# From a greedy schedule to a fixed order of all engines, with idle matmuls between the matmuls of the first two batches

## The chip, the cores and the metric

The kernel runs on one core of one Trainium2 chip. The metric is the device time of one execution in microseconds, as a median of several runs; lower is better. The engines are named as in the profile: PE (matmuls), PEld (its weight loads), DVE (vector), ACT (activations), POOL (GpSimd), SP (issues transfers). The kernels put matmul results into eight banks of PSUM, the accumulator memory. A run is called slow here when it is over 1.5% above the fastest run of the same kernel. Medians and ranges are of all runs; ratios and their intervals are of fast runs alone.

## The reference

Eight batches of eight heads: linear attention with an exponential feature map, then a gated unit with a causal convolution over five steps. The heart of it:

```python
def phi(x):                                    # x: (8, 8, 576, 64), w_phi: (64, 128)
    proj = np.einsum('bhsd,df->bhsf', x, w_phi)
    proj = proj - np.max(np.abs(proj), axis=-1, keepdims=True)
    return np.concatenate([np.exp(proj), np.exp(-proj)], axis=-1)
kv  = np.einsum('bhsf,bhsd->bhfd', phi(k), v)  # state
z   = np.sum(phi(k), axis=2)
x   = num / den                                # phi(q) kv / (phi(q) z + 1e-6), to (8, 576, 512)
gate = sigmoid(sum of 5 shifted x, each times conv_w[k])
out = (gate * (x @ w_val)) @ w_out             # (8, 576, 512) float32
```

## The kernel before

Every piece of work is a task with an engine, a duration from a table and a list of tasks it needs. A greedy scheduler simulates the engines when the kernel is built: whenever an engine is free, it takes the ready task of lowest priority number and, if the task opens a PSUM group, the first free bank or pair of banks.

```python
def run(self):                       # (cut)
    ...
    for e in engs:
        if free[e] > now + 1e-9:
            continue
        best = None
        for i in pend[e]:
            t = tasks[i]
            ...
            if best is not None and tasks[best].prio <= t.prio:
                continue
            g = t.grp
            if g is not None and t.opens:
                if nlive.get(g.kind, 0) >= self.live.get(g.kind, 8) or find(g.nb) is None:
                    continue
            best = i
    ...
    if e == "PE" and t.mode != mode:
        dur += 0.03
        mode = t.mode
```

The pieces that the change rewrites are the scaling of V by the k maxima on POOL (with masked copies where a block of rows straddles two heads), the state products, the gate, and the loads:

```python
def vs(self, t, b, g, s):            # POOL; (cut)
    for side in range(2):
        nc.gpsimd.tensor_tensor(EM[...], EK[...], MASK[...], ALU.mult)
    for a, st, n in ((1, 2, 4), (0, 8, 2)):
        nc.gpsimd.tensor_tensor(VT[:, s, sl, :, 0:D], Vg[:, sl, :, :], e..., ALU.mult)
    for side in range(2):
        nc.gpsimd.tensor_tensor(VB[:, s, :, :, side, 0:D], Vg[:, 2:7:2, :, :], e..., ALU.mult)

def rows(self, w, b):                # a 512-byte piece of q, k or v for each partition and y
    return self.src[w][b].rearrange("h (r t) d -> (h r) (t d)", t=2).rearrange("(y p) c -> p y c", p=P)
```

## Time and profile before

| | before |
|---|---|
| time, median (range) | 260.82 us (257.94 to 261.92) |
| profiled span, mean clock | 259.5 us, 0.916 |
| first exponential starts, last ends | 14.7, 231.1 us |
| first normalization of x in full blocks starts, last ends | 59.95, 238.5 us |

The lines that carry the reading stand in the prediction below. One more belongs here, the chain of work that ended last, by engine:

```profile
PE 52%; DMA 30%; DVE 10%; POOL 3%; issue 2%; ACT 1%; DVEq 0%; ACTq 0%; POOLq 0%
```

Three tenths of what set the end was data arriving: a load and transposing transfers of q.

### The profile page before, as it was taken

The numbers are of one execution on the slowest core, as the hardware profiler recorded it, in microseconds if no ns is written. First come the engines' busy times: TensorE is split into PE (matmuls) and PEld (weight loads), VectorE is DVE, ScalarE is ACT, GpSimd is POOL, SyncE is SP. The second block draws the span as 40 slices with busy tenths as digits, with TensorE's granted clock in tenths as the row PEclk, the third lists the DMA queues.
The fourth block names the chain that finished last, engine by engine and source line by source line (L and its number), as shares of the span: only waits on it lengthen the run. The fifth ranks groups of instructions, "written<-read, shape, count | busy, mean of one in ns | idle before, by whom it ended". The sixth has DMA issues, their size and how long they took to land.

```text
span 259.5 us, 8486 instructions
## 1 busy us (share of the span) xinstructions
PE 211.5 (81%) x3550; PEld 154.5 (60%) x3572; DVE 179.1 (69%) x284; ACT 187.1 (72%) x275; POOL 167.5 (65%) x364
## 2 busy tenths in 40 slices
PE   0464275588999999899984999899969999999982
PEld 0452153476776577667763677567747776677640
DVE  3373572687789888987893779877968799348320
ACT  1183389289888899898983898799869988563332
POOL 8880099799977797879494596767475747930000
PEclk9996555559999999999998899999999999999998
DMA  7999999999959996999999949981972002302205
GB/s 182 203 216 196 148 182 171 170 192 141 169 54 164 174 207 101 142 221 120 197 124 183 156 104 139 209 212 20 145 120 83 3 3 98 111 3 83 81 26 179
DMA packets 95760, 35.24 MB, mean 136 GB/s; under 512 B 84842, under 2 KB 91114, under 8 KB 95722
## 3 DMA queue, kind: packets, MB, share of 16 engines
q0 software_dynamic: 52624, 14.55, 57.3%
q1 hardware_dynamic: 42848, 20.06, 42.4%
q8 instruction: 28, 0.46, 0.8%
q10 hardware_dynamic: 250, 0.09, 0.1%
q14 instruction: 10, 0.08, 0.1%
HBM read 31.54 MB, written 9.44 MB: 158 GB/s over the span
## 4 chain that ended last, share of the span: by engine, by line
PE 52%; DMA 30%; DVE 10%; POOL 3%; issue 2%; ACT 1%; DVEq 0%; ACTq 0%; POOLq 0%
DMA qT<-KQN 20%; PE PS L754 12%; DMA KQN<-in_q_dram 10%; PE PS L775 9%; PE PS L742 8%; PE PS L551 7%; PE PS L621 6%; PE PS L663 3%; PE PS L668 2%; DVE GV L760 2%; DVE XN L708 2%; PE PS L716 2%; DVE MQP L558 2%; DVE GVT L765 1%; PE PS L684 1%
## 5 line engine op out<-in xcount | busy, mean ns | idle before, releaser
L568 ACT ACTIVATE KTIL<-PS 128x1024 bf16<-128x1024 f32 (+1 forms) x80 | 73.3, 943 | 12.0 <-PE PS L551 9.6
L674 ACT ACTIVATE QTIL<-PS 128x1024 bf16<-128x1024 f32 (+1 forms) x80 | 73.2, 947 | 11.7 <-PE PS L668 11.7
L558 DVE TENSOR_REDUCE MQP<-PS 128x8 f32<-128x1024 f32 (+1 forms) x40 | 44.1, 1114 | 17.4 <-PE PS L551 16.3
L588 POOL TENSOR_TENSOR VT<-VN,EK 128x512 bf16<-128x512 bf16 x64 | 53.3, 833 | 0.0
L593 POOL TENSOR_TENSOR VB<-VN,EM 128x384 bf16<-128x384 bf16 x64 | 52.7, 824 | 0.0
L558 DVE TENSOR_REDUCE MK<-PS 128x8 f32<-128x1024 f32 (+1 forms) x40 | 44.2, 1109 | 3.8 <-ACT KTIL L568 3.7
L754 PE MATMUL PS<-XT,WV 64*128 64x288 bf16 x512 | 37.1, 283 | 0.4
L760 DVE SCALAR_TENSOR_TENSOR GV<-TH,PS 128x576 bf16<-128x576 bf16 x32 | 24.1, 752 | 18.6 <-PE PS L754 15.7
L582 POOL TENSOR_TENSOR EM<-EK,MASK 128x6 f32<-128x6 f32 x64 | 11.4, 197 | 37.5 <-ACT EK L574 37.5
L775 PE MATMUL PS<-WOUT,GV 128*128 128x512 bf16 x106 | 30.8, 387 | 5.3 <-DVE XN L708 2.7
L635 ACT ACTIVATE OUTS<-PS 128x512 f32<-128x512 f32 x31 | 18.5, 597 | 17.7 <-PE PS L775 10.0
L621 PEld LDWEIGHTS <-KTIL 128*128 128x128 bf16 x640 | 27.7, 103 | 5.0 <-issue 3.3
L742 PE MATMUL PS<-XT,GT 128*64 128x288 bf16 x384 | 29.7, 290 | 0.0
L754 PEld LDWEIGHTS <-WV 64*128 64x128 bf16 x512 | 24.7, 94 | 7.5 <-issue 2.9
L746 ACT ACTIVATE TH<-PS 128x576 bf16<-128x576 f32 x32 | 21.2, 663 | 7.3 <-PE PS L742 5.6
L551 PE MATMUL PS<-W,qT 64*128 64x128 bf16 x288 | 17.4, 240 | 10.4 <-DMA qT<-KQN 8.6
L621 PE MATMUL PS<-VB,KTIL 128*128 128x130 bf16 (+1 forms) x256 | 22.0, 216 | 1.2 <-POOL VB L595 1.2
L708 DVE TENSOR_TENSOR XN<-PS,RCP 128x512 bf16<-128x512 f32 x32 | 22.1, 691 | 1.1
L742 PEld LDWEIGHTS <-GT 128*64 128x64 bf16 x384 | 18.9, 109 | 6.6 <-issue 3.2
L621 PE MATMUL PS<-VT,KTIL 128*128 128x65 bf16 x384 | 22.3, 200 | 0.5 <-ACT QTIL L674 0.5
L551 PE MATMUL PS<-W,kT 64*128 64x128 bf16 x288 | 16.0, 235 | 7.9 <-DMA kT<-KQN 4.6
L551 PEld LDWEIGHTS <-qT 64*128 64x128 bf16 x288 | 10.7, 104 | 18.0 <-DMA qT<-KQN 9.3
(64 smaller groups left out, 297.7 us busy)
## 6 DMA issues: line engine op xcount, KB each, us to landing
out_dram<-OUTS SPq DMA_DIRECT2D x32, 256.0 KB, 3.7
VN<-in_v_dram POOLq DMA_DIRECT2D x8, 576.0 KB, 11.8
KQN<-in_k_dram POOLq DMA_DIRECT2D x7, 576.0 KB, 9.6
KQN<-in_q_dram POOLq DMA_DIRECT2D x7, 576.0 KB, 15.4
QTIL<-in_k_dram SPq DMA_DIRECT2D x4, 256.0 KB, 4.1
WV<-in_moe_w_val_dram POOLq DMA_DIRECT2D x2, 512.0 KB, 14.0
QTIL<-in_q_dram SPq DMA_DIRECT2D x4, 256.0 KB, 12.1
out_dram<-OUTS SPq DMA_DIRECT2D x16, 64.0 KB, 2.3
```

Of the source, the lines that this page charges most:

```text
L551: nc.tensor.matmul(self.PS[:, t.grp.bank + par, i * P:(i + 1) * P], X[rows, (c0 + i) * P:(c0 + i + 1) * P], self.W2[rows, :], start=True, ...
L558: self.nc.vector.tensor_reduce(o, self.PS[:, t.grp.bank:t.grp.bank + 2, 0:n * P].rearrange("p a (c f) -> p a c f", f=F), AX.X, ALU.max, ap ...
L568: self.nc.scalar.activation(self.KTIL[b % 2][:, s, :, c0 * P:(c0 + n) * P], self.PS[:, t.grp.bank:t.grp.bank + 2, 0:n * P], AF.Exp, scale= ...
L588: nc.gpsimd.tensor_tensor(VT[:, s, sl, :, 0:D], Vg[:, sl, :, :], e.unsqueeze(3).to_broadcast([P, n, 2, D]), ALU.mult)
L593: nc.gpsimd.tensor_tensor(VB[:, s, :, :, side, 0:D], Vg[:, 2:7:2, :, :], e.unsqueeze(3).to_broadcast([P, 3, 2, D]), ALU.mult)
L621: nc.tensor.matmul(ps[:, col:col + E1 * len(mine)], self.KTIL[b % 2][:, s, par, c * P:(c + 1) * P], rhs, start=first, stop=True, skip_grou ...
L674: self.nc.scalar.activation(o, self.PS[:, t.grp.bank:t.grp.bank + 2, 0:n * P], AF.Exp, scale=1.0 - 2.0 * s)
L708: nc.vector.tensor_tensor(o.rearrange("p (g h) d -> p g h d", g=ng), n[:, :, :, 0:D], rc.unsqueeze(3).to_broadcast([P, ng, 4, D]), ALU.mult)
L742: nc.tensor.matmul(self.PS[h2 * D:(h2 + 1) * D, t.grp.bank + par, 0:R], self.GT[:, h, par, s, :], X[:, h, 2 - s:2 - s + R], start=(s == 0) ...
L754: nc.tensor.matmul(self.PS[:, t.grp.bank + par, 0:R], self.WV2[rows, h, j * P:(j + 1) * P], X[rows, h, 2:2 + R], start=(h == 0), stop=(h = ...
L760: nc.vector.scalar_tensor_tensor(out=self.GV[b % 3][:, j, :, :], in0=self.TH[j][:, :, :], scalar=1.0, in1=self.PS[:, t.grp.bank:t.grp.bank ...
L775: nc.tensor.matmul(self.PS[:, t.grp.bank, :], lhsT, self.WOUT[:, j, :], start=(j == 0), stop=(j == 3))
```

## The change

The intent of the last step, which gives the change its name, is to keep PE's clock up while the first two batches wait for data, by matmuls whose result nobody reads. The diff holds much more. The greedy scheduler gives way to fixed lists (an order of all tasks on all engines, a bank for each group, an engine for each movable copy), found offline. Cut to its core:

```diff
-PRM = dict(T=19.98, kp=(0.65, 4.21), ...)          # priorities
-LIVE = dict(kp=3, qm=2, ...)
+ORDER = ("15 16 18 17 20 19 22 21 24 35 23 37 ... ")  # 1064 tasks, all engines
+FLEX = ("ADAADAAAAAPPAPPD ... ")                      # ACT, DVE or POOL
+BANKS = ("460006544445500124166757 ... ")
+WARM = ("8:7:5 21:7:1 214:5:1 ")                      # place : bank : how many
...
-    def run(self):
-        ...                                           # greedy
+    def follow(self):
+        ...
+        return [self.tasks[int(i)] for i in ORDER.split()]
...
+    for i in range(NW):                               # 14 tasks of two idle matmuls
+        A("warm", 0, i, "PE", 0.44, fn("warm2"), [], plan.group("warm", 1), 0)
+    def warm(self, bank):
+        self.nc.tensor.matmul(self.PS[:, bank, :], self.ONES[:, 0:P], self.ONES[:, :], start=True, stop=True)
...
 def rows(self, w, b):
-    return self.src[w][b].rearrange("h (r t) d -> (h r) (t d)", t=2).rearrange("(y p) c -> p y c", p=P)
+    if w == "q":
+        return self.src[w][b].rearrange("h t d -> (h t d)").rearrange("(p x) -> p x", p=P)
+    return self.src[w][b].rearrange("(hp ab) (p j) d -> (ab p) hp (j d)", ab=2, j=9)
...
 def vs(self, t, b, g, s):                             # V: one product, no masks
+    eng.tensor_tensor(self.VT[g][:, s, :, 0:D], self.VN[b % 2][:, NC * g:NC * g + NC, :], e.to_broadcast([P, NC, D]), ALU.mult)
+    eng.tensor_copy(self.VT[g][:, s, :, D:E1], e)
...
 def st(self, t, b, g, x):                             # state: 64-row pairs, 144 a batch for 80
+    for ab in range(2):
+        rows = slice(ab * D, (ab + 1) * D)
+        nc.tensor.matmul(..., self.KTIL[b % 2][rows, s, J // 2, J % 2, :], self.VT[g][rows, s, 9 * x + j, :], ...)
```

Beside these: each of the gate's four parts takes 8 matmuls on the full height and half the width of the array (128 rows by 64 columns) and 4 on a quarter (64 by 64) instead of 12 of the former; V is loaded uncast through SP; the transposes of the convolution taps move behind the first k maxima; small copies on POOL hold back later loads; batch 1's q and k are transposed on PE; batches 6 and 7 transpose x by DMA; two load buffers instead of three, six output buffers instead of four.

## The prediction

> **What bounds the kernel now.** The few words that name the change fit only its last step; the diff replaces most of the kernel. So I first ask where 260 us go, starting with the page.
>
> ```profile
> span 259.5 us, 8486 instructions
> PE 211.5 (81%) x3550; PEld 154.5 (60%) x3572; DVE 179.1 (69%) x284; ACT 187.1 (72%) x275; POOL 167.5 (65%) x364
> ...
> ACT  1183389289888899898983898799869988563332
> ...
> PEclk9996555559999999999998899999999999999998
> DMA  7999999999959996999999949981972002302205
> ...
> DMA packets 95760, 35.24 MB, mean 136 GB/s; under 512 B 84842, under 2 KB 91114, under 8 KB 95722
> ```
>
> No engine is full: four lie between 167 and 212 us. ACT is thin in the first nine and last six slices, the TensorE clock is half in slices 5 to 9, and the DMA engines are full until three quarters of the span, with tiny packets. The busy-time windows put sizes on it (columns: PE, PEld, DVE, ACT, POOL busy, clock, DMA share, GB/s):
>
> ```profile
> 10.00:20.00 10.00, 7.42 (x65) 5.83 (x64) 7.75 (x18) 6.63 (x9) 7.30 (x4) 1.00 1.22 216
> 20.00:30.00 10.00, 4.64 (x38) 2.91 (x38) 5.07 (x6) 4.62 (x8) 0.00 (x0) 0.57 1.42 186
> 30.00:40.00 10.00, 5.84 (x67) 3.85 (x67) 5.58 (x7) 6.89 (x10) 7.03 (x16) 0.50 1.99 163
> 40.00:50.00 10.00, 4.31 (x57) 3.56 (x59) 3.47 (x4) 5.14 (x8) 8.21 (x20) 0.50 1.45 169
> ...
> sum 140.00, PE 128.02 PEld 94.12 DVE 114.67 ACT 119.54 POOL 103.95; mean PE 18.29 PEld 13.45 DVE 16.38 ACT 17.08 POOL 14.85
> ```
>
> The last line sums 60 to 200 us: there PE is busy 91% and ACT 85%. Before 60 us ACT works only 32.8 us (the rows above, 1.28 before and 8.27 after), so 27 are lost; after 200 us it works 34.7 of 59.5, so 25 more. The waits and the timeline say what the start waits for:
>
> ```profile
> PE PS L488 <- DMA cw<-in_moe_conv_w_dram: 9.7, 1, 9.7
> ...
> 15.89 3.81 ACT L568 ACTIVATE KTIL<-PS 128x1024 bf16<-128x1024 f32 x4
> ...
> 32.95 1.28 POOL L536 DMA_DIRECT2D KQN<-in_q_dram  x1 [14.12 <-DMA kT<-KQN]
> ```
>
> PE's first instruction stands behind a load of convolution taps until 9.7 us, though the timeline shows the k load issued at 0.74 us, and its issues land in about 4. POOL, which scales V, sits 14 us behind the transpose of the next k. In the chain of waits, 30% of the span is DMA (26.7 us of a q load from 8.2, then 12.2 of its transpose). By 47 us batch 0 has no state product; its first normalization comes at 60. In the middle it is a balance of engines under a greedy order. These groups price the work (busy, then mean ns):
>
> ```profile
> L568 ACT ACTIVATE KTIL<-PS 128x1024 bf16<-128x1024 f32 x64 | 64.5, 1029 | 10.7 <-PE PS L551 8.4 <-DVE MK L558 2.2
> L568 ACT ACTIVATE KTIL<-PS 128x512 bf16<-128x512 f32 x16 | 9.5, 595 | 1.3 <-PE PS L551 1.2
> L588 POOL TENSOR_TENSOR VT<-VN,EK 128x512 bf16<-128x512 bf16 x32 | 33.7, 1053 | 0.0
> L588 POOL TENSOR_TENSOR VT<-VN,EK 128x256 bf16<-128x256 bf16 x32 | 19.6, 613 | 0.0
> ```
>
> **What the Trainium skill says.** "TensorE: Matmul & The Clock Gate", Part 1: the array clock halves after about 3.4 us of idling and returns after as long a busy window. The trace agrees: 0.50 between 30 and 50 us, where PE is busy 43 to 58%, and 1.00 in the busy stretch after 60. The same page, Part 3: matmuls on different row or column groups of the array run concurrently. It agrees: 16 value matmuls of 64 rows and 288 columns take 0.99 us in the chain, 62 ns each, where one of 512 columns takes 216 to 240. "DMA: Bandwidth & Descriptors", Specifications: at least 512 B is needed for line rate. Here 89% of packets (84842 of 95760) are smaller, and the engines are full at about 190 GB/s. "GPSIMD Engine Reference", 3.1: about 2.6 cycles an element at 1.2 GHz for two inputs on GpSimd. Here (1053-613)/256 = 1.72 ns, 2.1 cycles; I use the measured slope.
>
> **The change part by part.** Counts are from the two compiled instruction orders.
>
> *Start.* The tap transposes go behind the first batch's k maxima, POOL's loads wait for the fourth k load, V comes uncast through SyncE and q, k in long rows (q 9.2 KB a partition instead of 512 B). PE can start transposing k when it has landed, near 4 us, not 10.65; ACT near 5.5, not 11.8: 6 us. Batch 1's q and k are transposed on PE rather than by DMA. I expect most of the other 20 lost microseconds of the start to go too.
>
> *Idle matmuls.* 35 of 128x512: five ahead of PE's first transposes, one in the first projections, 28 as 14 pairs in the ordered list between the matmuls of batches 0 and 1, one more behind them. At 0.22 us each (the pace of the 512-column output matmuls) they are 7.7 us of PE, mostly in holes. They buy clock: in the chain, PE pieces from 47 to 59 us, some 9 us at half speed, would have been about 4.5 shorter, an upper bound since batch 0 waits more for data.
>
> *ACT* (the x4 row: (3.81-1.03)/3 = 0.93 us from start to start, 0.10 less than a duration). 128 wide exponentials x 0.93 = 119; 16 half ones x 0.50 = 8; 32 quarter ones (estimate from the slope, 0.28) = 9; 32 tanh x 0.56 = 18; 22 of 36 output evictions x 0.50 = 11 (31 before); KV copies, EK and start copies about 10. Sum 175, against 181 counted so before. ACT's gain is in its idle time, not its work.
>
> *DVE.* 64 wide reductions x 1.12 = 72, 16 half ones 9, gated products 21, normalization 27, x copies 12, 24 evictions 14, the rest 8: 163. The gather copies of q and output remainders leave it.
>
> *POOL.* V is scaled in one product of 1152 elements: 1152 x 1.72 + 173 = 2.15 us plus a copy of 0.2, 31 times = 73; loads, taps, halo and gather copies about 35. So 108 instead of 167; no longer a rival.
>
> *PE per batch*, from chain and timeline pieces at full clock: projections 72 in eights of 0.33 = 3.0; q features 2.5; state 3.1; numerator 2.4; x transposes 1.35; gate 4 x 0.86 = 3.4; value 4 x 1.0; output 18 x 0.23 = 4.1; the rest 0.2: 24. Changed: state products go from 80 (64 of 65 columns, 16 of 130) to 144 half-height ones of 65 columns in concurrent pairs: 72 x 0.03 (the numerator's pace, 48 in 1.4 us) = 2.2, say 2.3; gate from 12 to 8 full plus 4 quarter-array ones, 0.86 x 8/12 + 0.12 = 0.69, so 2.8. New: 22.6 a batch, 181 in all, less 2 where batches 6 and 7 transpose x by DMA, plus 7.7 idle.
>
> *Order.* A fixed list with fixed PSUM banks replaces the greedy scheduler. The list puts all exponentials before the last stretch; after the last q features, PE still has about 0.6 state, 5.5 gate, 2.7 numerator, 8 value and 8 output: 25 us.
>
> **The sum.** ACT starts at 5.5, does 175 less about 7 in the tail = 168, with 6% idle = 10 (15% before); then PE's 25 less 2.5 overlapped by the last exponentials; then eviction 0.6 and landing 2.0: 5.5+168+10+22.5+2.6 = 208.6. PE check: 179 real microseconds between 4.5 and 206 is 89%, as in the old middle (91%), so it fits. I say **208 us**, 20% less.
>
> **Rivals.** (1) Data still comes late: 12 big DMA transposes remain, and in the old trace they take 10 to 14 us to land. Against: that was under saturation, and short packets go. If so, the start loses 10 again and the period stays DMA-bound: 220 to 225. (2) A fixed list is only as good as its timings: one late operation stalls a whole in-order queue, and ACT, PE and DVE now have nearly equal loads (175, 187, 163). At the old 15% idle ACT gives 227. For it: no slack between equals; against: the banks and engines were chosen together. (3) The idle matmuls lie on PE's path, or fail to hold the clock: 3 to 5 us more. (4) The order is tight and ACT loses 2%: 201; with less tail 198. A slower kernel would need the DMA change to fail outright; nothing speaks for it.
>
> **Range and chances.** (4) bounds the low side, most of (1) and (2) the high side: 198 to 220 holds eight in ten. Within 2% of 260 would take 47 us of error, so faster 0.98, same 0.01, slower 0.01.
>
> **What would show it.** Right: first k transposes before 6 us and first exponential before 8; PEclk 9 in slices 3 to 9; packets well under 95760, DMA below 9 in the middle; ACT busy about 175 to 180 of its span, 93% until its last exponential; POOL under 120; the last q exponential about 25 us before the end, PE full after it. Wrong: ACT windows at 85% in the middle with waits on PE (rival 2) or on qT, kT transposes (rival 1); a clock still half in the first quarter (rival 3); a tail over 30 us.

## The result, and the profile after

The changed kernel took 230.04 us in the median (229.07 to 230.28, four runs) beside 260.82 us for the kernel before. The ratio is 0.8845, with a 95% interval of 0.8761 to 0.8929. Ratios here are the mean time of one kernel's fast runs over that of the other's of the same rounds, so not quite the ratio of the medians. The direction was right. The time lies outside the predicted range of 198 to 220, and 22 us above the predicted 208.

First the page of the changed kernel, the lines that answer to those shown of before:

```profile
span 228.5 us, 9138 instructions
PE 205.4 (90%) x4001; PEld 142.6 (62%) x4027; DVE 176.3 (77%) x264; ACT 180.7 (79%) x266; POOL 102.8 (45%) x158
...
ACT  2995999889899988988899999979988999913220
...
PEclk9997999999999999999999999999999999999998
DMA  6999943999699939995899995969964206156156
...
DMA packets 49282, 39.87 MB, mean 174 GB/s; under 512 B 33690, under 2 KB 38554, under 8 KB 49178
...
PE 53%; DVE 17%; DMA 4%; issue 3%; ACT 3%; POOL 2%; DVEq 0%; ACTq 0%
```

The start is repaired: ACT is busy from the second slice on, the clock is up in all but the fourth slice until the last, packets are half as many, and data is 4% of the chain that ended last, not 30%. DMA is still at 9 in many slices, though, and that did not hurt.

Next, the first and the last normalization of x in full blocks, first the two of before, then the two of after (start, duration, engine, line):

```profile
59.95 0.69 DVE L708 TENSOR_TENSOR XN<-PS,RCP 128x512 bf16<-128x512 f32 x1
...
237.85 0.69 DVE L708 TENSOR_TENSOR XN<-PS,RCP 128x512 bf16<-128x512 f32 x1
```

```profile
40.70 0.69 DVE L691 TENSOR_TENSOR XN<-PS,RCP 128x512 bf16<-128x512 f32 x1
...
202.66 0.69 DVE L691 TENSOR_TENSOR XN<-PS,RCP 128x512 bf16<-128x512 f32 x1
```

These split the gain of the profiled spans, 259.5 - 228.5 = 31.0 us. Up to the first normalization 19.2 are won. From the first to the last start it took 177.9 us before and 162.0 after: 15.9 more. From there to the end it took 21.6 before and 25.8 after: 4.2 lost again. (Their sum, 30.9, is the gain but for rounding.)

The busy-time windows of after (PE, PEld, DVE, ACT, POOL busy, then clock, DMA share, GB/s) show the stages:

```profile
0.00:20.00 20.00, 13.35 (x133) 8.41 (x134) 11.99 (x15) 13.49 (x22) 8.49 (x17) 0.97 0.92 265
20.00:40.00 20.00, 17.12 (x333) 10.68 (x336) 14.27 (x18) 18.42 (x26) 14.40 (x24) 0.95 0.73 152
40.00:60.00 20.00, 16.87 (x410) 12.64 (x409) 17.63 (x27) 17.46 (x26) 11.63 (x14) 1.00 1.11 198
60.00:180.00 120.00, 115.96 (x2383) 82.46 (x2391) 102.53 (x155) 107.28 (x156) 56.72 (x81) 1.00 0.86 187
```

From 60 to 180 us ACT is busy 89.4%, not the 93% expected, while PE is busy 97% by the records. ACT's longest waits from 60 us to its last q exponential at 198.2 us (waiting engine and line, what ended the wait, then us in total, times, longest):

```profile
ACT TH L743 <- PE PS L739: 3.4, 8, 0.7
ACT KTIL L572 <- PE PS L555: 2.6, 5, 1.1
ACT QTIL L657 <- PE PS L649: 2.4, 7, 0.6
```

All name PE: its gate, its projections and its q features. With two smaller ones it is 10.5 us on PE, of the 13.8 that ACT is idle in this stretch. No wait of any engine is put down to a transfer there. The tail itself, from ACT's last q exponentials over PE's last output products:

```profile
194.31 3.88 ACT L657 ACTIVATE QTIL<-PS 128x1024 bf16<-128x1024 f32 x4
```

```profile
221.31 1.89 PE L775 MATMUL PS<-WOUT,GV 128*128 128x512 bf16 x8
```

The exponentials end at 198.2 us, PE ends at 223.2, and the span 5.3 us later.

**How full PE really was.** The records of matmuls overlap (in run 14 a 64-column one lasts 0.19 us and the next starts 0.01 us after it), so a PE that waits a little can look full. Starts are better. I went through PE's tasks in the trace, priced each at the shortest start-to-start time of its kind, added 0.1 us wherever PE passed between forms (half rows, full array, half columns; the reason comes with the experiments), and counted no task for longer than it took. So reckoned, PE was occupied 18.2 us of the first 35 (52%), 17.9 of the next 25 (72%), and 108.5 of the 120 from 60 to 180 (90%). This is an estimate, and the trace lacks some records, 6 of the 35 idle matmuls among them. A recount by groups of like matmuls, on this trace and that of run 5, gives 21 to 26 us of the first 35 (16 to 19 without the idle matmuls), 18 of the next 25 and 107 to 110 of the 120.

### The profile page after: what moved, and what is told of

Read it like the earlier page. It is cut to its first block, busy times and chain, and to the rows that moved or that the text cites. A ratio compares the mean times of both kernels' runs of the same rounds, so it can differ in the third digit from the quotient of the medians.

```text
span 228.5 us, 9138 instructions
## 1 busy us (share of the span) xinstructions
PE 205.4 (90%) x4001; PEld 142.6 (62%) x4027; DVE 176.3 (77%) x264; ACT 180.7 (79%) x266; POOL 102.8 (45%) x158
## 4 chain that ended last, share of the span: by engine, by line
PE 53%; DVE 17%; DMA 4%; issue 3%; ACT 3%; POOL 2%; DVEq 0%; ACTq 0%
PE PS L751 13%; PE PS L775 10%; PE PS L732 7%; PE PS L598 5%; PE PS L555 5%; DVE XN L691 4%; DMA kT<-KQN 4%; DVE MQP L562 3%; PE PS L670 3%; DVE MK L562 3%; PE PS L739 3%; DVE GV L757 2%; PE PS L642 2%; PE PS L699 2%; PE PS L649 2%
## 5 line engine op out<-in xcount | busy, mean ns | idle before, releaser
L588 POOL TENSOR_TENSOR VT<-VN,EK 128x1152 bf16<-128x1152 f32 x31 | 65.8, 2123 | 60.2 <-ACT EK L581 50.8
L657 ACT ACTIVATE QTIL<-PS 128x1024 bf16<-128x1024 f32 x64 | 62.6, 1036 | 4.6 <-PE PS L649 4.0
L751 PEld LDWEIGHTS <-WV 64*128 64x128 bf16 x512 | 24.6, 94 | 8.3 <-issue 2.6
L598 PE MATMUL PS<-VT,KTIL 64*128 64x65 bf16 x1152 | 24.1, 191 | 1.4 <-POOL VT L589 0.5
L598 PEld LDWEIGHTS <-KTIL 64*128 64x128 bf16 x1152 | 21.3, 95 | 4.2 <-issue 1.3
L670 PE MATMUL PS<-KV,QTIL 128*128 128x65 bf16 x512 | 20.1, 193 | 1.7 <-DVE GV L757 0.5
L670 PEld LDWEIGHTS <-QTIL 128*128 128x128 bf16 x512 | 18.2, 97 | 5.0 <-issue 2.7
L612 ACT ACTIVATE OUTS<-PS 128x512 f32<-128x512 f32 x22 | 13.3, 606 | 9.8 <-PE PS L775 9.1
L732 PE MATMUL PS<-XT,GF 128*64 128x288 bf16 x256 | 20.6, 290 | 0.4 <-DVE MQP L562 0.2
L775 PEld LDWEIGHTS <-GV 128*128 128x128 bf16 x128 | 11.0, 97 | 11.6 <-issue 1.1
L642 PE MATMUL PS<-qT,W 64*128 64x512 bf16 (+1 forms) x80 | 15.0, 359 | 0.9 <-ACT QTIL L657 0.5
```

The costliest lines, as they stand in the source:

```text
L588: eng.tensor_tensor(self.VT[g][:, s, :, 0:D], self.VN[b % 2][:, NC * g:NC * g + NC, :], e.to_broadcast([P, NC, D]), ALU.mult)
L598: nc.tensor.matmul(self.PS[:, t.grp.banks[ab], (s * 2 + x) * E1:(s * 2 + x + 1) * E1], self.KTIL[b % 2][rows, s, J // 2, J % 2, :], self.V ...
L657: self.nc.scalar.activation(o, i, AF.Exp, scale=1.0 - 2.0 * s)
L670: nc.tensor.matmul(self.PS[:, t.grp.banks[h // 4], (h % 4) * E1:(h % 4 + 1) * E1], Q[:, s, c % 2, h, (c // 2) * P:(c // 2 + 1) * P], self. ...
L732: self.nc.tensor.matmul(self.PS[h2 * D:(h2 + 1) * D, t.grp.banks[par], 0:R], self.GF[:, h, i, :], X[:, h, :, HALO - 8 * s:HALO - 8 * s + X ...
L751: nc.tensor.matmul(self.PS[:, t.grp.banks[par], 0:R], self.WV2[rows, h, j * P:(j + 1) * P], X[rows, h, :, HALO:XW], start=(h == 0), stop=( ...
```

## The experiments

Eighteen kernels ran. Unless said, each is the changed kernel with one edit, and is compared with its 230.0 us.

### Idle matmuls

**1. No idle matmuls.** `warm` returns at once; order and banks stay.

```diff
     def warm(self, bank):
+        return
```

> The changed kernel without its 35 idle matmuls, nothing else touched (right result). If they hold the clock and batches 0 and 1 need it: the clock drops to a half in the first quarter and the time rises by 3 to 5 us. If they only lie on PE's path: the time falls by up to 5 us. If both balance or neither matters: within 1 us of 230. My guess is 232.

Measured: 232.42 us (231.44 to 233.37), ratio 0.9003 (0.8919 to 0.9086), about 2 us longer. The windows of this kernel, then one of the changed kernel:

```profile
30.00:40.00 10.00, 5.49 (x174) 4.65 (x167) 5.37 (x7) 8.94 (x14) 6.17 (x6) 0.76 0.40 102
40.00:50.00 10.00, 8.85 (x183) 7.47 (x184) 9.09 (x18) 7.66 (x12) 6.01 (x9) 0.73 1.13 209
```

```profile
30.00:40.00 10.00, 8.18 (x220) 5.58 (x222) 6.66 (x8) 10.00 (x15) 6.72 (x7) 1.00 0.31 75
```

The idle matmuls hold the clock at 1.00 where it would be 0.73 to 0.76. They are worth 2 us of the 31 that the whole change gains.

**2. Idle matmuls in the kernel before.** One 512-column idle matmul goes ahead of each of the first 45 PSUM groups.

```diff
+            if left and t.eng == "PE" and t.opens and t.fn is not None:
+                left -= 1
+                em.idle(t.grp.bank)
```

> The kernel before with one idle matmul ahead of each of the first 45 PSUM groups that PE opens, its order untouched (right result). If the half clock cost the old start 4 us, as I put it at most: 2 to 4 less and the clock full before 50 us. If the old start waits for data: within 1, whatever the clock.

Measured: 264.05 us, ratio 1.0079 (0.9983 to 1.0175). The clock rose from 0.916 to 0.958 and the time did not fall. That fits a start that waits for data.

### Is it the order?

**3. The new operations under the old scheduler.** The changed kernel's tasks, no idle matmuls, ordered by the greedy scheduler with the old priorities.

```diff
-        for i, t in enumerate(plan.follow()):
+        for t in plan.run():         # with PRM, LIVE and the run() of the kernel before
```

> The operations of the changed kernel, without idle matmuls, ordered by the greedy scheduler and the priorities of the kernel before (right result). If the fixed order carries the gain: near the old 85% of ACT with the new start, 240 to 255. If the changed operations and loads carry it and the order little: within 5 us of 230.

Measured: 291.7 us, ratio 1.1287 (1.1169 to 1.1406). The same operations without idle matmuls take 232 us (run 1) or 292 according to their order, their banks and the engines chosen for movable copies. (The priorities were tuned for the old operations, so this is no fair verdict on greedy scheduling.)

**4. One part alone in the kernel before.** The tap transposes move behind the first k maxima.

```diff
-    cc = A("mqt", 0, 0, "PE", 0.5, fn("c_cw"), (), g, prio=-500)
+            cc = A("mqt", 0, 0, "PE", 0.5, fn("c_cw"), [G("kmax", 0, 4)], g, prio=-500)
```

> The kernel before, with its tap transposes behind the first batch's k maxima as in the changed kernel (right result). If PE's late start costs what I counted: 4 to 6 us less than before. If the start is held by q, V and the next batch's loads anyway: 0 to 2 us less.

Measured: 269.81 us, ratio 1.0453 (1.0349 to 1.0557). The first exponential came at 8.5 us instead of 14.7, and yet the kernel is slower: the greedy order reshuffled itself around the edit (ACT's instructions differ in 194 of 275 places). Which part of the new order costs the time isn't shown. Parts of this change can't be added up one by one under that scheduler.

### Which engine's work counts?

In each of these an engine's work is cut, with a wrong result where said.

**5. The changed kernel again**, as a partner for the next ones.

> The changed kernel again, unaltered, so that it stands beside the next three on the same chip: 229 to 231 us.

Measured: 230.31 us (230.21 to 231.39), ratio 0.895 (0.8893 to 0.9006).

**6. Value products over four of eight heads** (wrong result): 16 us less for PE.

```diff
-        for h in range(H):
+        for h in range(H // 2):
```

> The changed kernel with the value product over 4 of 8 heads (wrong result on purpose): 256 matmuls, 16 us, less on PE, 2.5 of them in the tail per batch 7 and 6 groups. If PE binds throughout: 14 to 16 us less. If no engine binds and hand-offs in the fixed order do: 5 to 9 less, about half of it in the tail.

Measured: 223.07 us, ratio 0.8652 (0.8557 to 0.8746): 7 us shorter, less than half of what was taken away, which is what was expected "if no engine binds". In the profiled run, the slowest of the four, the last q exponential ends at 195.3 us instead of 198.2: 2.9 us earlier, though six of eight batches, some 12 of the 16 us, lie before it.

**7. Maxima over half the features** (still within the tolerance): 38 us less for DVE.

```diff
-            o, ...rearrange("p a (c f) -> p a c f", f=F),
+            o, ...rearrange("p a (c f) -> p a c f", f=F)[:, :, :, 0:F // 2],
```

> The changed kernel with the k and q maxima over half of the features (wrong result on purpose): 64 reductions shorter by 0.53 us and 16 by 0.27, 38 us less on DVE. If DVE binds: over 25 us less. If nearly equal loads in fixed queues wait on one another: 8 to 15 less, since the reductions also hold PSUM and gate the scaling of V. If DVE is a bystander: within 2.

Measured: 227.5 us, ratio 0.8817 (0.8753 to 0.888); the three fast runs took 226.73 to 228.14: 3 us shorter.

**8. tanh over 64 of 576 elements** (still within the tolerance): 14 us less for ACT.

```diff
-        self.nc.scalar.activation(self.TH[j][:, :, :], self.two(t.grp, R), AF.Tanh)
+        self.nc.scalar.activation(self.TH[j][:, :, 0:32], self.two(t.grp, 32), AF.Tanh)
```

> The changed kernel with tanh over 64 instead of 576 elements (wrong result on purpose): 32 x about 0.43 = 14 us less on ACT. If ACT binds up to its last exponential: 12 to 14 less. If no engine does: 4 to 7 less. If PE alone binds: within 2.

Measured: 232.57 us (229.05 to 235.0), ratio 0.8928; the two fast runs took 229.05 and 231.19 us: nothing gained. The windows from 60 to 180 us, of the run with less for PE, then of the run with less for ACT:

```profile
60.00:180.00 120.00, 112.65 (x2329) 77.44 (x2327) 105.13 (x159) 110.90 (x163) 57.62 (x86) 1.00 0.88 189
```

```profile
60.00:180.00 120.00, 117.03 (x2410) 82.90 (x2408) 103.00 (x155) 99.82 (x157) 57.40 (x84) 1.00 0.88 187
```

With less for PE, ACT fills up to 92.4%. With less for ACT, ACT idles more (83%) and PE is as before. In this stretch ACT follows PE, but PE alone does not set the pace either, since most of the 16 us did not come back.

**9. All three cuts together** (wrong result).

> Half value product, half maxima and short tanh together (wrong result on purpose): PE 16, DVE 38, ACT 14 us less. If three nearly equal engines wait on one another: clearly more than the largest single one of the three, 20 to 30 less than the changed kernel. If the remaining time is hand-off latency alone, which none of these cuts: no more than 10 less.

Measured: 219.99 us, ratio 0.8531 (0.8488 to 0.8574): 10 us shorter, though 16, 38 and 14 us of work are gone. What is then left is not the load of one engine. By the expectation ("no more than 10 less") this is about where hand-offs alone would leave it.

### Is it data?

**10. A third load buffer**, q alternating between two, and POOL no longer waiting before it loads.

```diff
-        bufs = TT("KQN", 2, [P, NC, 2 * D])
+        bufs = TT("KQN", 3, [P, NC, 2 * D])
-                self.N[w][b] = bufs[i]
+                self.N[w][b] = bufs[1] if w == "k" else bufs[2 * (b % 2)]
```

> The changed kernel with a third buffer for the loaded q and k (q alternates between two) and without POOL's wait for the previous q transpose before it issues the next loads; the convolution taps rest in a GV buffer to make room (right result). The weak answers to shorter maxima and tanh suggest another pace: load k, transpose k, transpose q, wait, load, 21 to 24 us a batch. If that cycle sets the pace: loads issue up to 5 us earlier in it and the time falls by 5 to 12. If data comes early enough as it is: within 2 of 230.

Measured: 230.18 us (229.32 to 231.04), ratio 0.8796 (0.8724 to 0.8867). But the edit did not do what it was to do: POOL issues each load of q and k within 0.7 us of where it did before the edit. One load of q, in the changed kernel and in this one:

```profile
94.56 0.61 POOL L528 DMA_DIRECT2D KQN<-in_q_dram  x1
```

```profile
95.03 0.60 POOL L528 DMA_DIRECT2D KQN<-in_q_dram  x1
```

So this run says nothing about earlier loads.

**11. The same with all three cuts** (wrong result).

> The three cuts (value product, maxima, tanh) with the same deeper loading (wrong result on purpose). If the load and transpose cycle held the three cuts at 220: now 200 to 208. If hand-offs of the fixed order hold them: within 3 of 220.

Measured: 220.17 us, ratio 0.8414 (0.8351 to 0.8477), as without the buffer. Here too most loads are issued where run 9 issues them (91.98 and 91.58 us, 111.88 and 111.77), so it tests no more than run 10.

**12. A quarter of V** from batch 2 on (wrong result): for those batches 7 MB of loads become less than 2.

```diff
+        h = 4 if b < 2 else 1
-        self.nc.sync.dma_start(..., self.rows("v", b))
+        self.nc.sync.dma_start(...[:, 0:h, :], self.rows("v", b)[:, 0:h, :])
```

> The changed kernel that loads a quarter of V from batch 2 on (wrong result on purpose): 5.3 MB less of 39.9, which the q and k loads need not share engines with. If DMA throughput binds: 5 or more less. If not: within 2 of 230.

Measured: 229.61 us, ratio 0.8773 (0.8708 to 0.8837). Less traffic does not move the time. It also settles a point of the start. In the changed kernel the chain that ended last holds one long transfer, the transpose of batch 2's k (8.90 us from 37.11). Here it is issued earlier, first the changed kernel, then this run:

```profile
37.11 5.51 SPq L543 DMA_TRANSPOSE kT<-KQN  x1
```

```profile
32.83 3.17 SPq L544 DMA_TRANSPOSE kT<-KQN  x1
```

PE's next k projections still start at 46.10 us (46.06 in the changed kernel), and the chain no longer passes through a transfer there. The loads look like a pace in the trace, with transposing transfers close behind their loads, but my theory of a loading cycle has nothing left for it: from 60 to 198.2 us no engine's wait in the changed kernel is put down to a transfer. A run that really loads earlier was not made.

### What PE's changes of form cost

The trace shows a projection on half rows followed after 0.036 us by another half-row matmul, but after 0.146 us by one on the full array. The fixed order has 204 changes of form, 162 of them between 64 and 128 rows and the others in columns, and its table allows 0.05 us for each. (The kernel before has 188 by the same count.) Two runs put needless 64-column matmuls at the same 60 places, on the full array or on half rows.

**13. Full array: 86 more changes of form.**

```diff
+        if b >= 2:
+            nc.tensor.matmul(self.PS[:, t.grp.banks[0], 0:D], self.ONES[:, 0:P], self.ONES[:, 0:D], start=True, stop=True)
```

> The changed kernel with one needless matmul of 64 columns on the full array ahead of each of the 60 k and q maxima groups of batches 2 to 7, which are on half rows and mostly follow work on half rows; it goes into the group's own bank and is overwritten. It adds about 86 changes between half rows and the full array. If each costs PE the 0.1 us read from the trace (0.146 us from a half-row projection to a full-array matmul against 0.036 us to another half-row one), PE gets some 10 us more, and the replay of the trace's durations gives 5 to 6 us longer: 235 to 236. If changes cost nothing, as the next run.

**14. Half rows: no more changes.**

```diff
+        if b >= 2:
+            nc.tensor.matmul(self.PS[:, t.grp.banks[0], 0:D], self.ONES[0:D, 0:P], self.ONES[0:D, 0:D], start=True, stop=True)
```

> Control for the run before: the same 60 needless matmuls of 64 columns at the same places, but on 64 rows, so that no change between half rows and the full array is added. By the trace's pace 60 x 0.03 us = 1.8 us more for PE: 230 to 231.5. If it is as slow as the run with full-array matmuls, the change of form is not what costs.

Measured: 238.22 us (237.91 to 240.34) with the full array, ratio 0.9201 (0.908 to 0.9322); 230.74 us (230.12 to 234.08) on half rows, ratio 0.8902 (0.8784 to 0.9021); its three fast runs have a median of 230.43. PE's timeline at one such place, full array, then half rows (start, duration, engine, line):

```profile
133.28 0.74 PE L600 MATMUL PS<-VT,KTIL 64*128 64x65 bf16 x36
133.96 0.20 PE L553 MATMUL PS<-ONES 128*128 128x64 bf16 x1
134.09 0.40 PE L557 MATMUL PS<-W,kT 64*128 64x128 bf16 x8
```

```profile
127.93 0.75 PE L600 MATMUL PS<-VT,KTIL 64*128 64x65 bf16 x36
128.51 0.19 PE L553 MATMUL PS<-ONES 64*128 64x64 bf16 x1
128.52 0.41 PE L557 MATMUL PS<-W,kT 64*128 64x128 bf16 x8
```

Read the starts. From the state products to the projection it is 133.28 to 134.09, 0.81 us, against 127.93 to 128.52, 0.59 us: two changes cost 0.22 us (the needless matmul stands in both). The busy column would have shown next to nothing. Over the kernel, 7.8 us between the fast runs (238.22 - 230.43) for 86 changes is 0.09 us each. Two things follow. First, the 204 changes of the order as it stands are some 20 us of PE's time (204 x 0.1, an estimate; it takes the 42 changes in columns to cost as much). Second, of the time added to PE in batches 2 to 7, 86 x 0.11 = 9.5 us by the timeline, some 80% comes out at the end: PE has little slack there. The Trainium skill names a cause in "TensorEngine Tiling (Array Packing)", section Key Properties: changing the tiling mode, not just the tile, drains the TensorE. The runs agree that a change takes time and add the number; that a drain is what takes it they don't show. I had not looked that page up for the prediction.

### Another order of the same operations

If hand-offs laid down by the order hold back the rest, another order should win it. I replayed the order with durations and hand-offs read from the trace (0.21 us from PE to ACT, 0.25 us to DVE, 0.14 us from a bank's last reader to PE, 0.1 us a change of form). The replay followed the trace of the changed kernel at a constant distance of about 1.3 us from 20 us on. Then I searched for an order that was shorter in this replay.

**15. New lists with the measured hand-offs**, and **16. the same search with the table's own constants**, as a control. Only `ORDER`, `BANKS`, `FLEX` and `WARM` differ.

```diff
-ORDER = ("15 16 18 17 20 ...")
+ORDER = ("...")                      # the same 1064 tasks
-BANKS = ("4600065444455...")
+BANKS = ("...")                      # pairs no longer always neighbours
```

> The changed kernel with every operation kept and only the fixed lists new: another order of the same operations on PE, ACT, DVE, POOL and the queues, other PSUM banks, other choices of engine for the movable copies. The lists come from a search over orders whose length was reckoned from durations read in the changed kernel's trace: start-to-start times of each operation, 0.21 us from a PE result to ACT, 0.25 us to DVE, 0.14 us from the last reader of a bank to PE, and 0.1 us whenever PE passes between matmuls on half rows and on the full array (204 such changes in the order as it stands). The changed kernel's own order, reckoned so, follows the trace with a constant offset of about 1.3 us from 20 us to the end. Theory 1 (the idle time of ACT lies in the hand-offs and changes that this order lays down): 8.5 us less than the changed kernel, 221 to 223 (an estimate from those durations). Rival (another cause, a transfer or an engine's real load, sets the pace): no change, 229 to 231; or longer, as happened when the old kernel's order was disturbed.

> Control for the run before: the same search for the same time, but with the durations and hand-offs written in the changed kernel's own tables (0.17 us for every hand-off, 0.05 us for a change of PE's form). If the wrong constants are why the order came out long, this one should gain clearly less than the reordered kernel. If a longer or different search is what gains, it comes out near it: reckoned with the measured durations it is 6.8 us shorter than the changed kernel, so 223 to 225 (an estimate).

Measured: 379.29 us and 368.86 us, ratios 1.4657 and 1.4199: both failed by some 140 us and more, with correct results. The waits of run 15 (waiting engine and line, releaser, then us in total, times, longest):

```profile
DVE MK L562 <- ACT KTIL L572: 34.9, 23, 6.0
...
ACT KTIL L572 <- DVE MK L562: 20.5, 16, 3.0
```

DVE and ACT wait for each other, though both only read what PE wrote. The replay lacked two waits. In these traces two engines that read one bank take turns: the Trainium skill, "PSUM — Partial Sum Buffer", section PSUM bank collisions raise a hardware error, says that the compiler back end's scheduler adds a dependency between any two instructions on different engines that touch the same bank and quadrant, reads included; the trace agrees, with DVE starting 0.03 us after ACT's end. And, as I infer from the replay, an operation on two banks that are not neighbours also waits for the banks between them; no run tests this alone, and it may be the bookkeeping of the framework that builds the program and not the chip. All pairs of the changed kernel are neighbours; mine were not. With both waits in, the replay gives 372 us for run 15 and 361 us for run 16, where the profiled spans are 375.9 and 366.4, and still 225.5 for the changed kernel.

**17 and 18. The same two searches with these waits**, pairs neighbours again.

> The reordered kernel again, after the failed run showed which two waits the reckoning lacked: an operation on two PSUM banks that are not neighbours also waits for the banks between them (all pairs of the changed kernel are neighbours, the failed order's were not), and two engines that read one bank take turns. With these two waits in, the replay of the trace's durations gives the failed order 372 us against the 376 of its profile, and the changed kernel 225.5 as before. The new search keeps pairs to neighbouring banks and has both waits. All operations are those of the changed kernel; changes between half rows and full array fall from 204 to 192. Theory 1 (the time lies in hand-offs and changes that the order lays down): the replay is 8 us shorter than that of the changed kernel, so 221 to 223 (an estimate). Rival (another cause): 229 to 231. Should it be far longer again, the reckoning still lacks a wait and the theory stays open.

> Control: the same search, the same two rules, but with the durations and hand-offs of the changed kernel's own tables (0.17 us for every hand-off, 0.05 us for a change of PE's form) in place of the measured ones. Replayed with the measured durations it is 2.4 us longer than the other new order and 5.4 us shorter than the changed kernel: 223.5 to 225.5 (an estimate). As fast as the other: the search gains, the constants don't. At 229 to 231: only the measured constants gain.

Measured: 235.13 us (233.64 to 235.8), ratio 0.902 (0.8938 to 0.9102), and 232.36 us (230.68 to 233.7), ratio 0.8928 (0.8813 to 0.9042). Neither is faster than the changed kernel. PE's timeline of run 17 at the places where it fell behind its replay:

```profile
25.18 1.03 PE L533 MATMUL PS<-ident,QTIL 128*128 128x128 bf16 x8 [3.18 <-DMA QTIL<-in_k_dram]
```

```profile
148.62 1.04 PE L775 MATMUL PS<-WOUT,GVT 128*128 128x512 bf16 x4 [1.26 <-POOL GVT L763]
```

Batch 1's k landed about 7 us later than the replay had it, and by 33 us the kernel was 9 us behind. From there to 140 us it kept that distance within about 2 us, then lost some 3 us more by 165 around POOL's copy and the outputs. So the replay had the loads wrong first of all. Whether an order exists that wins the 8 us stays open: these two did not test it, because they brought in their own late data. No kernel of this study that computes the whole reference beats the changed one.

## Why the prediction was right or wrong

The sum of the prediction and the trace of the changed kernel, term by term:

| term | predicted, us | measured, us |
|---|---|---|
| ACT starts | 5.5 | 5.5 |
| ACT's work up to its last q exponential | 168 | 172.5, busy by the records |
| ACT idle in that time | 10 (6%) | 20.2 (198.2 - 5.5 - 172.5) |
| PE after it | 22.5 | 25.0 (223.2 - 198.2) |
| eviction and landing | 2.6 | 5.3 |
| sum | 208.6 | 228.5 (profiled span) |

**The step that failed** is "with 6% idle = 10", together with the check that was to secure it: "179 real microseconds between 4.5 and 206 is 89%, as in the old middle (91%), so it fits." ACT was idle 20.2 us (10%), 6.4 of them before 60 us and 13.8 after, and most of its waits after 60 us were on PE. (At the shortest start-to-start times ACT's work is 163 us and its idle time 29; the step is the same.) The PE check missed it because it spread PE's work, idle matmuls included, evenly from 4.5 us on. By 60 us it needs (60 - 4.5) x 0.905 = 50 us of PE. (0.905 is the 187 us priced in all, less 25 of the tail, over the 179 from 4.5 to 183.5.) My count gives PE 36.1 us there, the recount 39 to 43, of which 7 to 8 are idle matmuls. So PE was 7 to 14 us behind the check at 60 us, and at 90% from there on it could not catch up. That is 7 to 14 of the 14.7 us by which the last q exponential came late (198.2 instead of 183.5); what the rest is stays open. The amount of PE work was about right: 162 us predicted before the tail, 159 counted up to 196 (160 to 168 in the recount). Some of that is luck: the recount holds about 19 us for changes of form, which the prediction did not price apart, though the old pieces that it priced from held changes too.

The mechanism behind it, as I read it, is that PE has too little to do at first. From 5.5 to 60 us ACT is busy 48.1 of 54.5 us, 88%, with exponentials of batches 0 and 1 above all, while PE can't yet do the numerators, gates, values and outputs that need them. Later PE is nearly full and ACT waits on it. ACT's own share is much the same in both stages (88%, then 90%); it is PE's that changes, and this part is argued from the windows. The runs show for the middle that some 80% of the work added to PE comes out at the end (runs 13 and 14), that work taken from PE gives 7 of 16 us and fills ACT to 92.4%, and that work taken from ACT gives nothing. They also show what speaks against PE as the one cause: with all three engines relieved only 10 us come back. That more PE work in the first 60 us would bring the 7 to 14 us back was not tested. Nor is all of PE's own 10% of waiting explained.

**Smaller misses.** ACT's work was 4.5 us more by the records, which is less than the ways of counting differ by. The tail of PE was 2.5 longer. Eviction and landing took 5.3 instead of 2.6: outputs now take 0.56 us each in the median to issue on SP, where they took 0.33 before, and they queue at the end.

**Points that held.** The first k transposes came at 3.84 us and the first exponential at 6.6. The clock stood at 9 in slices 3 to 9 but for the fourth slice. Packets fell to 49282. POOL's product of V took 2.12 us (2.15 predicted) and POOL was busy 102.8 us. ACT's busy sum was 180.7. PE was full after the last exponential (24.6 of 25.0 us).

**Points that did not.** DMA did not fall below 9 in the middle, and run 12 shows that it need not. ACT was not 93% busy to its last exponential. The tail was 30.3 us from that point, just over the 30 that I had named as a sign of error. And the trace agrees only in part with what the prediction took from the skill about the clock: it halved without 3.4 us of idling (the closing list has the figures).

**The rivals.** Late data (220 to 225): in the middle no wait is put down to a transfer, and run 12 gains nothing from less traffic or from an earlier transpose of batch 2's k. Runs 10 and 11 do not count, since their loads did not move. Stalls of a fixed list at 15% idle (227) came nearest in number and in sign (ACT waiting on PE), but what kept PE busy was partly a cost that I had not priced apart, 204 changes of form. Hand-offs of the list stay a rival for the rest: runs 6 and 9 came out as expected for them, and runs 17 and 18 did not decide it. Idle matmuls in the way: no, they gain 2 us.

## What to carry to other kernels

Price an engine stage by stage: an average over the whole span hides that an engine has little to do early and is full later. Read PE by the starts of its matmuls, not by the length of their records, and count how often it passes between row-tiled and full-array matmuls. Before trusting a replay of a schedule, let it predict a schedule that fails. After an edit, look in the trace whether it moved what it was to move: run 10 did not.

## What the Trainium skill lacked or had wrong

- "TensorEngine Tiling (Array Packing)", Key Properties, says that a change of tiling mode drains the TensorE but gives no duration. Here a change between 64-row and full-array matmuls cost 0.09 us over the kernel (7.8 us for 86) and 0.11 us in the timeline (0.22 for two). With 204 changes in 230 us it was some 8 to 9% of PE's time (an estimate).
- "TensorE: Matmul & The Clock Gate", Part 1, gives an idle window of about 3.4 us before the clock halves, but not how much work a window may hold. Here the clock halved at 21.5 and 140.9 us in the kernel before, at 18.7 in the changed kernel and at 25.0 and 35.2 in run 1, each time without 3.4 us of idling: in the 3.4 us before, PE was busy 21 to 61% by the records (10 to 51% without transposes), and its longest gaps were 0.7 to 2.7 us. Nor is a held clock a gain by itself: 0.73 to 0.76 against 1.00 for 20 us was worth 2 us of 230 in one kernel, and nothing in the other (0.916 to 0.958, 264.05 against about 261 us).
- "PSUM — Partial Sum Buffer", the section on bank collisions, agrees with ACT and DVE taking turns on a bank (34.9 and 20.5 us of waits in run 15). It does not say what a pair of banks that are not neighbours costs: two orders with such pairs took 379.29 and 368.86 us, and replays that also wait for the banks between come within 6 us of their spans. Whether that wait is the chip's is not shown.
- "DMA: Bandwidth & Descriptors": I found no figure there for what issuing a store costs SP by its access pattern. Here one output store took 0.56 us in the median to issue, and 0.33 us in the arrangement of the kernel before.
- I found no page with hand-off times between the engines. Here, from the end of one record to the start of the instruction that waited for it, the median was 0.04 us from PE to ACT or DVE and 0.05 us from ACT or DVE to PE. Counted from the last start plus its start-to-start time, as in my replay, they were 0.21, 0.25 and 0.14 us, because a record lasts longer than the pace (0.10 us on ACT).
